# State factors by a product with a 0/1 matrix instead of through DRAM, and a planner that puts wide products between thin ones, in a kernel of linear attention and two dense layers

## The chip, the core and the metric

The kernel runs on one core of a Trainium2 chip. That core has a tensor engine (PE) for matrix products into PSUM, a vector engine (DVE), a scalar engine (ACT), GpSimd (POOL), and a queue on SyncE (SP) from which every transfer of this kernel is issued, in the order of the program. The metric is the time of one launch on the device in microseconds; lower is better.

## What is computed

A linear attention with complex decays feeds a first dense layer, and that a second one. Batch 4, 8 heads, 768 tokens, 48 channels a head; 384 channels in all; hidden widths 2048 and 1536.

```python
mag = np.sqrt(a_re * a_re + a_im * a_im)
scale = np.minimum(mag, 0.999) / (mag + 1e-06)
for t in range(S):
    new_re = ar * S_re - ai * S_im        # ar, ai: the scaled decays of token t
    new_im = ar * S_im + ai * S_re
    S_re, S_im = new_re + einsum('bhd,bhe->bhde', k[t], v[t]), new_im
    y[:, :, t] = einsum('bhd,bhde->bhe', q[t], S_re)
x = y as (tokens, channels)
h = x @ w_in;  x = (h * sigmoid(1.702 * h)) @ w_out              # first layer
g = x @ w_gate;  x = (silu(g) * (x @ w_val)) @ w_out             # second layer
```

## The kernel before, in words

**Tiling.** The attention goes in chunks of 128 tokens. A *unit* is two chunks of one batch, so there are twelve units, u0 to u11, three to a batch; u2, u5, u8 and u11 are the last of theirs. For a unit, DVE and ACT work out running complex products of the decays (`decays`, `products`), then scale queries and keys by them (`queries`: the tile `qh`; `keys`: the line `p<-p,kr`, the last step on DVE). Both go to DRAM (`dq`, `dk`) and come back with the heads' rows in the partitions (`sq`, `sk`; `stack` and `load_heads`). On PE a chunk then takes: transposes of the keys (`kt`), scores (`sc`, 8 heads, in two groups of four, `masked`), the result (`y`, lines 592 and 594, `heads`), its transposes (`xp`, `turn_x`, which make the layer's input `xt`) and what the chunk adds to the state (`ds`). These have 48 or 128 columns and are called *thin* here. At a unit's end the state `M` is multiplied by a real factor for each row of each head, the tile `tots`. The factors `mag` (`passed_on`) lie with channels in the partitions; they go to DRAM as `md` and are read back as `tots`, once for the real and once for the imaginary half.

**The layers.** Weights come as float64 words, which DVE and ACT turn into two float32r parts. For the first 32 blocks of weights the second part is made on PE (lines 773 and 774, an *early pair*). The first layer (`layer_one`) takes 256 tokens, one unit, at a time: 16 blocks `h` of nine products, and 16 blocks `acc` of nine, each `acc` three blocks behind its `h`; between them ACT and DVE make `gs` (`gelu`). The second layer works on 512 tokens at a time (`pg`, `pv`, `o`). The products of both layers have 256 to 512 columns and are called *wide*.

**What sets the order.** `Plan` is a list scheduler that runs while the program is written. Each row of work is a generator that says which engine its next step takes and for how long, and which events or buffer places it waits for. Of the steps that could start first, the one with the smallest urgency number is written next. The numbers come from a table (`URGENCY`, `EXTRA` for each unit, `RUSH`, `W_FIRST`, `SPILL`, `NEAR`). Its times are estimates, and on the chip only the order remains: every engine runs its instructions in that order, and waits where an input is not there. In the program before, a transfer's estimate is 1.3 times its bytes over 360 GB/s plus 3.7 us, a block of nine wide products of 256 columns 1.005 us, and `y` of one chunk is two steps of 1.66 us, between which other work may be put.

```python
for g in range(2):
    yield at[g]
    ...
    yield pe(0.79 if first else 1.66)
    for h in range(4):
        T.matmul(y[:, hs], at[g].x[:, h], u.v[:, c, hs], start=True, stop=first)
        if not first:
            T.matmul(y[:, hs], u.sq[:, 4 * g + h, cols(c)], old[:, hs], start=False, stop=True)
```

Of the kernel before, what the change touches and what calls it, by code (L numbers as in the profile page):

```python
# [30 lines left out]
class Slots:  # L31
    """Places for tiles of one tag, with the times at which they fall free."""
# [5 lines left out]
class Plan:  # L38
    """Puts rows of steps in one order for all engines.

    A row (a generator) asks for what its next step needs: (engine, us), an Event, or Slots; it is
    resumed, and then issues the step. Of the steps that could start first, the one of the most
    urgent row is taken. The times are estimates and only the order rests on them.
    """

    # from the end of a step to the start of one that waits for it
    LAT = {"PP": 0.0, "VP": 0.25, "AP": 0.25, "PV": 0.2, "VV": 0.13, "AV": 0.14, "PA": 0.2, "VA": 0.13, "AA": 0.22}
    # some durations (and those of transfers) are taken long: the order then has slack for them
    SLACK = {"A": 1.05, "V": 1.03}

    def __init__(self):
        self.free = dict(P=0.0, V=0.0, A=0.0, S=0.0, D=0.0)
        self.rows = []
        self.now = 0.0
        self.n = 0
        self.warm = 0.0
        self.table = None
        self.row = [0, 0, None, [], None, "S", NEAR]

    def add(self, urgency, gen, after=False, near=None):  # L60
# [46 lines left out]
    def run(self, until=None):  # L107
        while self.rows and (until is None or until.time is None):
# [4 lines left out]
            for row in self.rows:  # L113
                if isinstance(row[4], tuple):
                    turn = row[4][2:] and row[4][2] != self.table
# [11 lines left out]
            start = self.ready(row, SWITCH if row[4][2:] and row[4][2] != self.table else 0.0)  # L127
            if engine == "P":
                # the tensor engine's clock is at half speed after a pause
                if start - self.free["P"] > (0.5 if start < self.warm else 2.0):  # L130
                    self.warm = start + 3.4
                if start < self.warm:
                    us *= 2
            self.free[engine] = self.now = start + us
# [5 lines left out]
def vec(n):  # L140
    return "V", 0.065 + n / 960
# [6 lines left out]
def act2(n, *table):  # L148
    """Two, the second on what the first gave."""
    return "A", 0.44 + n / 600, *table  # L150

# [4 lines left out]

ISSUE = ("S", 0.48)
NEAR = 0.094
SWITCH = 1.3
TURN = 1018.0  # L160
NEAR0 = [0.129, 0.005]
# [3 lines left out]
class Attention:  # L165
    """Linear attention with complex decays, in chunks of 128 tokens.

    With P[t] the product of a chunk's decays up to t, times the phase of all that came before it
    in the batch, q[t] * P[t] and k[s] / P[s] give the chunk's scores by one product, and the state
    passes from chunk to chunk by real factors (powers of two near the chunk's decay; the phase  # L170
    takes up the rest). A unit is a few chunks of a batch. Channels (h, d) lie in the partitions, in
    NT tiles.
    """

    def __init__(self, nc, plan, const, sb, ps, xs, dram, flag, q, k, v, a_re, a_im, H):
# [10 lines left out]
        make_upper_triangular(nc, self.mask)  # L186
        self.G = None
# [5 lines left out]
    BUFS = dict(p=4, big=2, m2=1, r=1, x=1, d2=1, kr=1, qk=2, v=1, s=1, kn=2, at=2, m=2, sc=2, xt=2, mag=2, tots=1)  # L193
# [4 lines left out]
    def start(self, units):  # L198
        """The rows of work of all units: (batch, first chunk, chunks)."""
        add = self.plan.add  # L200
        for i, (b, c0, n) in enumerate(units):
# [5 lines left out]
                                        "sq", "sk", "tots", "kn", "x", "phase", "md")}  # L207
# [10 lines left out]
    # ---- loads  # L218
# [29 lines left out]
    # ---- decays: a / (|a| + 1e-6) * min(|a|, 0.999)  # L248
    def decays(self, u):
# [11 lines left out]
        # (the logarithm's domain is 2 ** -64 to 2 ** 64)  # L261
# [32 lines left out]
    def root(self, u):  # L294
        """Of the decays' squares."""
# [9 lines left out]
    def inverse(self, u):  # L305
        """Of the products' squares."""
# [9 lines left out]
    # ---- products of the decays over the chunk  # L316
    def cmul(self, out, x, y, shape):
        """out = x * y over complex pairs [128, 2, *shape] (x and y may be broadcast)."""
        V = self.nc.vector
        n = 1  # L320
# [11 lines left out]
        else:  # L332
            full = [128, 2, 2] + list(shape)
            yield vec(4 * n)
# [12 lines left out]
    def products(self, u, last):  # L347
# [8 lines left out]
        # over the blocks of eight: in fours, then over the fours  # L356
# [13 lines left out]
        # G[.., c] is the phase at the start of chunk c of the unit  # L370
# [10 lines left out]
        # the product up to the start of each block of eight  # L381
# [8 lines left out]
        # joined with the products within the blocks  # L390
# [865 lines left out]
```

## Time and profile before

| | |
|---|---|
| median of 3 runs | 1167.28 us (1163.76 to 1175.69) |
| span of the profiled execution | 1167.8 us |
| PE busy | 1096.8 us (94%) |
| PE weight loads | 1015.9 us (87%) |
| DVE busy | 728.8 us (62%) |
| ACT busy | 554.0 us (47%) |
| bytes moved | 103.54 MB, mean 89 GB/s |
| chain that ended last | PE 86%, DMA 7%, DVE 4%, ACT 2% |

Busy is the time in which an engine has an instruction at work. PEclk is the clock that TensorE was granted, as a share of 2.4 GHz; 0.5 is 1.2 GHz. In a list of waits, "PE h L786 <- ACT g" means that PE's instruction of line 786 stood idle until ACT's instruction had written `g`.

### The profile page before, as it was taken

How to read it: one execution, taken by the hardware profiler on the slowest of the kernel's cores; microseconds unless marked ns; L12 is line 12 of the kernel's file. 1: busy time of each engine (PE TensorE's matmuls, PEld its weight loads, DVE VectorE, ACT ScalarE, POOL GpSimd, SP SyncE). 2: the span in 40 equal slices, each digit the busy share in tenths (PEclk: the TensorE clock that was granted, in tenths of full speed). 3: DMA queues.
4: the chain of work that ended last, by engine and by line, in shares of the span. 5: the costliest groups of instructions: out<-in, count | busy, mean ns of one | idle time of the engine just before them, and what ended most of it. 6: DMA issues, size and time to landing. Idle time of an engine off the chain costs nothing.

```text
span 1167.8 us, 18608 instructions
## 1 busy us (share of the span) xinstructions
PE 1096.8 (94%) x7312; PEld 1015.9 (87%) x7312; DVE 728.8 (62%) x1638; ACT 554.0 (47%) x1279; POOL 1.1 (0%) x8
## 2 busy tenths in 40 slices
PE   1549899999999999999999999999999999999996
PEld 0228889999999999999999999888888888888886
DVE  6999988889788998888862599622231231322221
ACT  7987545667447656644442699422121121211211
POOL 0000000000000000000000000000000000000000
PEclk9569999999899999999999999999999999999999
DMA  9770715618257263525813664001010010000000
GB/s 329 251 162 15 164 54 136 159 46 150 82 136 135 70 123 95 122 56 109 163 58 72 211 221 145 27 2 54 1 55 1 1 55 1 28 1 1 28 1 30
DMA packets 101391, 103.54 MB, mean 89 GB/s; under 512 B 14001, under 2 KB 95410, under 8 KB 101298
## 3 DMA queue, kind: packets, MB, share of 16 engines
q1 hardware_dynamic: 101298, 102.29, 34.8%
q8 instruction: 59, 0.97, 0.3%
q14 instruction: 34, 0.28, 0.1%
HBM read 73.95 MB, written 28.32 MB: 88 GB/s over the span
## 4 chain that ended last, share of the span: by engine, by line
PE 86%; DMA 7%; DVE 4%; ACT 2%; issue 1%; SPq 0%; DVEq 0%; ACTq 0%
PE h L786 6%; PE h L788 5%; PE h L787 5%; PE acc L786 5%; PE acc L787 5%; PE acc L788 5%; PE o L1005 4%; PE o L1006 4%; PE o L1007 4%; PE pg L787 4%; PE pv L787 4%; PE pv L786 4%; PE pg L788 4%; PE pg L786 4%; PE pv L788 4%; PE sc L559 4%
## 5 line engine op out<-in xcount | busy, mean ns | idle before, releaser
L975 DVE TENSOR_TENSOR s<-s,pv 128x512 f32<-128x512 f32 x72 | 49.5, 687 | 236.0 <-PE pv L788 234.9
L786 PE MATMUL h<-xt,w 128*128 128x256 f32 x576 | 170.0, 295 | 7.8 <-ACT g L841 6.4
L786 PE MATMUL acc<-gs,w 128*128 128x256 f32 x576 | 169.0, 293 | 0.0
L787 PE MATMUL h<-xt,w 128*128 128x256 f32 x576 | 164.8, 286 | 0.6 <-DVE xt L661 0.6
L787 PE MATMUL acc<-gs,w 128*128 128x256 f32 x576 | 164.5, 286 | 0.4 <-DVE gs L847 0.4
L788 PE MATMUL h<-xt,w 128*128 128x256 f32 x576 | 164.5, 286 | 0.0
L788 PE MATMUL acc<-gs,w 128*128 128x256 f32 x576 | 164.5, 286 | 0.0
L839 ACT ACTIVATE gs<-h 128x256 fp32r<-128x256 f32 x192 | 73.8, 384 | 148.7 <-PE h L788 147.3
L972 ACT ACTIVATE s<-pg 128x512 f32<-128x512 f32 x72 | 43.0, 598 | 174.4 <-PE pg L788 174.4
L786 PEld LDWEIGHTS h<-xt,w 128*128 128x128 f32 x576 | 111.8, 194 | 10.8 <-ACT g L841 8.3
L787 PEld LDWEIGHTS h<-xt,w 128*128 128x128 f32 x576 | 111.9, 194 | 1.0 <-DVE xt L661 1.0
L786 PEld LDWEIGHTS acc<-gs,w 128*128 128x128 f32 x576 | 111.9, 194 | 0.7
L787 PEld LDWEIGHTS acc<-gs,w 128*128 128x128 f32 x576 | 111.8, 194 | 0.7 <-DVE gs L847 0.6
L788 PEld LDWEIGHTS h<-xt,w 128*128 128x128 f32 x576 | 111.8, 194 | 0.0
L847 DVE TENSOR_TENSOR gs<-g,gs 128x256 fp32r<-128x256 f32 x192 | 80.6, 421 | 49.8 <-ACT g L841 48.8
L788 PEld LDWEIGHTS acc<-gs,w 128*128 128x128 f32 x576 | 111.6, 194 | 0.0
L980 ACT CAST p<-s 128x512 fp32r<-128x512 f32 x72 | 44.7, 621 | 130.5 <-DVE s L975 130.5
L1005 PE MATMUL o<-w,p 128*128 128x384 f32 x288 | 97.2, 338 | 0.0
L1006 PE MATMUL o<-w,p 128*128 128x384 f32 x288 | 97.2, 337 | 0.0
L1007 PE MATMUL o<-w,p 128*128 128x384 f32 x288 | 97.1, 337 | 0.0
L787 PE MATMUL pg<-xs,w 128*128 128x512 f32 x216 | 85.1, 394 | 0.0
L787 PE MATMUL pv<-xs,w 128*128 128x512 f32 x216 | 84.7, 392 | 0.0
(128 smaller groups left out, 2448.9 us busy)
## 6 DMA issues: line engine op xcount, KB each, us to landing
words<-in_moe_w_out_dram SPq DMA_DIRECT2D x28, 384.0 KB, 8.4
dq<-qh SPq DMA_DIRECT2D x24, 384.0 KB, 8.9
dk<-p SPq DMA_DIRECT2D x24, 384.0 KB, 6.9
sq<-dq SPq DMA_DIRECT2D x24, 384.0 KB, 7.2
sk<-dk SPq DMA_DIRECT2D x24, 384.0 KB, 8.5
words<-in_moe_w_in_dram SPq DMA_DIRECT2D x16, 384.0 KB, 8.4
p<-in_a_re_dram SPq DMA_DIRECT2D x12, 384.0 KB, 3.8
p<-in_a_im_dram SPq DMA_DIRECT2D x12, 384.0 KB, 4.7
```

What stands on the lines that cost most here:

```text
L559: T.matmul(sc[:, h], u.sk[:, 4 * g + h, cols(c)], u.sq[:, 4 * g + h, cols(c)], start=True, stop=True)
L786: T.matmul(out, w[:, 0, ws], xh, start=start, stop=False)
L787: T.matmul(out, w[:, 0, ws], xl, start=False, stop=False)
L788: T.matmul(out, w[:, 1, ws], xh, start=False, stop=stop)
L839: A.activation(gs[:, 0], h, AF.Gelu_apprx_sigmoid)
L847: V.tensor_tensor(out=gs[:, 1], in0=g, in1=gs[:, 0].bitcast(F32), op=ALU.subtract)
L972: A.activation(s, gv[0], AF.Silu)
L975: V.tensor_tensor(out=s, in0=s, in1=gv[1], op=ALU.mult)
L980: A.copy(p2[:, 0], s)
L1005: T.matmul(os[i], p2[:, 0, cols(i)], w[:, 0], start=f == 0, stop=False)
L1006: T.matmul(os[i], p2[:, 0, cols(i)], w[:, 1], start=False, stop=False)
L1007: T.matmul(os[i], p2[:, 1, cols(i)], w[:, 0], start=False, stop=f == F2 - 1)
```

## The change

It has four parts.

1. **The factors stay on the chip.** Two constants are made on POOL at the start: `rows`, a 0/1 matrix that sends a channel's partition to its row (d, or 48 + d) in the heads' layout, and `mine`, which is 1 where a channel belongs to a head. `passed_on` multiplies `mine` by `mag` on DVE (`own`, bf16, exact since the factors are powers of two), PE multiplies by `rows` (three products of 8 columns into `tp`, each with a weight load of its own), and ACT copies the result to `tots`. The transfers `md<-mag` (one a unit) and `tots<-md` (two a unit) are gone, in the eight units that are not a batch's last.
2. **Wide between thin.** `y` and `ds` are marked as thin steps. The planner adds up the thin time in a row, and where the next thin step would bring it over a limit, it writes another PE step first, if one can start within 0.5 us. Its own estimate of when PE runs at half speed is changed too: from pauses to how much work, thin steps counting for little, it has put there lately.
3. **Other durations.** Transfers are taken at 366 GB/s and 2.5 us, at 1.75 times that for `sq` and `sk`; a block of nine products at 1.08 us; `y` at 1.79, `ds` at 1.36, a group of `sc` at 0.9.
4. **Another table of urgencies**, and the places of weights in SBUF are given out in the order in which they fall free.

```diff
@@ Plan
-    def load(self, event, size):
-        self.free["D"] = max(self.free["D"], self.now + 0.6) + size * 1.3 / 360e3
-        self.set(event, self.free["D"] + 3.1 - self.now)
+    def load(self, event, size, slow=1.0):
+        self.free["D"] = max(self.free["D"], self.now) + size * slow / 366e3
+        self.set(event, self.free["D"] + 2.5 - self.now)
...
+            if row[4][3:] and self.few and self.few + row[4][1] > FEW - 0.6:
+                other = [x for x in ready if x[3][4][0] == "P" and not x[3][4][3:] and x[0] < start + 0.5]
+                if other:
+                    row = min(other, key=lambda x: x[1:3])[3]
...
+                thin = row[4][3:]
+                self.few = (self.few if start - self.free["P"] < 0.3 else 0.0) + us if thin else 0.0
@@ Attention.passed_on
-            yield slots["mag"]
             yield vec(NT)
-            mag = self.tile("mag", [128, NT])
+            mag = sb.tile([128, NT], F32, tag="mag", name="mag", bufs=1)
...
-            yield ISSUE
-            u.md = self.dram.tile([self.HD, 1], F32, tag="md", name="md", bufs=2)
-            self.nc.sync.dma_start(out=u.md.rearrange("(j p) c -> p j c", p=128), in_=mag[:, :, None])
-            plan.set(u.ev["md"], 4.0)
+            if u.c0:
+                yield self.units[u.i - 1].ev["tots"]
+            yield vec(NT * self.H)
+            own = sb.tile([128, NT, self.H], BF16, tag="own", name="own", bufs=1)
+            V.tensor_tensor(out=own, in0=self.mine, in1=mag[:, :, None].to_broadcast([128, NT, self.H]), op=ALU.mult)
+            yield slots["tots"]
+            yield slots["m"]
+            yield pe(0.6)
+            tp = self.tile("m", [128, 512], name="tp", pool=self.ps)[:2 * self.D, :self.H]
+            for j in range(NT):
+                self.nc.tensor.matmul(tp, self.rows[:, j].rearrange("p e d -> p (e d)"), own[:, j],
+                                      start=j == 0, stop=j == NT - 1)
+            yield act(self.H)
+            u.tots = self.tile("tots", [2 * self.D, self.H, 1])
+            A.copy(u.tots[:, :, 0], tp)
@@ Attention.load_heads
-        if not self.last(u, u.n - 1):
-            yield u.ev["md"]
-            yield slots["tots"]
-            yield ISSUE2
-            u.tots = self.tile("tots", [2 * D, H, 1])
-            for e in range(2):
-                self.nc.sync.dma_start(out=u.tots[e * D:(e + 1) * D], in_=u.md.rearrange("(h d) c -> d h c", d=D))
@@ Attention.heads
-                yield pe(0.79 if first else 1.66)
+                yield thin(0.9 if first else 1.79)
...
-                yield pe(1.29)
+                yield thin(1.36)
@@ layer_one, layer_one_out
-                yield pe(9 * N / 2400 + 0.045)
+                yield pe(9 * (N / 2400 + MM))
@@ the table, two of its lines
-W_FIRST, W_STEP = 284.7, 16.205
+W_FIRST, W_STEP = 1731.0, 11.064
```

**Where instructions move.** Lines of the changed kernel have numbers some 50 higher: 592 and 594 (`y`) are 639 and 641, 786 to 788 (the wide products) 835 to 837, 773 and 774 (the early pair) 822 and 823, 742 and 745 (two passes over a weight's words) 790 and 793.

First, PE at the first chunk of u2, where the result of the first four heads ends and that of the other four begins (`at` is the masked scores of one group). Before:

```order
L592 MATMUL y_2054<-v_1629,at_2040 128x48
L594 MATMUL y_2054<-M_1621,sq_1790 128x48
L592 MATMUL y_2054<-v_1629,at_2063 128x48
L594 MATMUL y_2054<-M_1621,sq_1790 128x48
L592 MATMUL y_2054<-v_1629,at_2063 128x48
```

Now, at the same chunk:

```order
L639 MATMUL y_2089<-v_1649,at_2071 128x48
L641 MATMUL y_2089<-M_1636,sq_1758 128x48
L835 MATMUL h_2105<-xt_1494,w_897 128x256
L836 MATMUL h_2105<-xt_1494,w_897 128x256
L837 MATMUL h_2105<-xt_1494,w_897 128x256
...
L639 MATMUL y_2089<-v_1649,at_2085 128x48
L641 MATMUL y_2089<-M_1636,sq_1758 128x48
```

A block of nine wide products has come between the two groups. Before, all 20 chunks that take up a state run their 16 products of `y` without a break; now one of the 20 does, the second chunk of u0.

Second, ACT at the very start, in the decays of u0 (`x` and `r` of 768 columns) and the first weights (`junk`). Before:

```order
L302 ACTIVATE r<-r 128x768
L742 ACTIVATE junk,flags<-words 128x384
L269 ACTIVATE x,flags<-r 128x768
L745 ACTIVATE junk,flags<-junk 128x384
L742 ACTIVATE junk,flags<-words 128x384 x2
L745 ACTIVATE junk,flags<-junk 128x384
L278 ACTIVATE x<-r 128x768
```

Now:

```order
L346 ACTIVATE r<-r 128x768
L313 ACTIVATE x,flags<-r 128x768
L790 ACTIVATE junk,flags<-words 128x384 x2
L793 ACTIVATE junk,flags<-junk 128x384 x2
L322 ACTIVATE x<-r 128x768
L302 ACTIVATE sq,flags<-p 128x1536
L324 ACTIVATE r<-r 128x768
```

The first `x` has moved ahead of the first weight; the second `x` (278, now 322) stands behind two weights' four passes, and the squares of u1 (`sq`) ahead of the last `r`.

Third, PE just before the first wide product, at the end of u0's second chunk. Before:

```order
L773 MATMUL h<-r,ident 128x384
L774 MATMUL h<-w,minus 128x384
L773 MATMUL h<-r,ident 128x384
L774 MATMUL h<-w,minus 128x384
L654 MATMUL xp<-ident,ysb 128x128 x3
L611 MATMUL ds<-v,kn 96x48 x8
L773 MATMUL h<-r,ident 128x384
L774 MATMUL h<-w,minus 128x384
L786 MATMUL h<-xt,w 128x256
```

Now:

```order
L822 MATMUL h<-r,ident 128x384
L823 MATMUL h<-w,minus 128x384
L701 MATMUL xp<-ident,ysb 128x128 x3
L658 MATMUL ds<-v,kn 96x48 x8
L822 MATMUL h<-r,ident 128x384
L823 MATMUL h<-w,minus 128x384
L835 MATMUL h<-xt,w 128x256
```

One early pair has gone from ahead of `xp` to a place further up; there are 32 pairs in both.

## Rows read from the trace of the kernel before

**Rows 1.** Stages: us, busy time of each engine (instructions), PEclk, DMA share, GB/s.
```profile
0.00:84.00 84.00, 33.28 (x63) 15.11 (x63) 70.71 (x173) 71.61 (x200) 1.14 (x8) 0.68 0.83 250
104.50:640.00 535.50, 524.50 (x4370) 518.31 (x4368) 447.46 (x1066) 291.96 (x643) 0.00 (x0) 0.97 0.49 106
640.00:1158.00 518.00, 518.00 (x2741) 464.54 (x2741) 191.44 (x346) 176.00 (x406) 0.00 (x0) 1.00 0.14 47
```
**Rows 2.** The same view, the 10 us in which the granted clock falls.
```profile
140.00:150.00 10.00, 8.09 (x54) 7.47 (x52) 7.31 (x22) 1.55 (x4) 0.00 (x0) 0.83 0.33 86
165.00:175.00 10.00, 7.93 (x51) 7.20 (x49) 9.93 (x18) 6.31 (x12) 0.00 (x0) 0.83 0.46 155
200.00:210.00 10.00, 8.60 (x65) 8.47 (x65) 7.04 (x15) 6.40 (x12) 0.00 (x0) 0.83 0.02 0
250.00:260.00 10.00, 10.00 (x78) 10.00 (x78) 8.07 (x14) 6.38 (x14) 0.00 (x0) 0.83 0.14 41
300.00:310.00 10.00, 10.00 (x65) 10.00 (x65) 5.47 (x13) 3.05 (x8) 0.00 (x0) 0.66 0.01 2
505.00:515.00 10.00, 10.00 (x73) 10.00 (x72) 6.50 (x16) 4.80 (x13) 0.00 (x0) 0.83 0.14 39
630.00:640.00 10.00, 10.00 (x80) 10.00 (x79) 2.83 (x5) 1.72 (x5) 0.00 (x0) 0.83 0.01 2
```
**Rows 3.** The same view, one run of y and the stretch behind it.
```profile
248.90:252.40 3.50, 3.50 (x35) 3.50 (x33) 3.50 (x6) 2.05 (x5) 0.00 (x0) 0.99 0.00 0
252.40:255.80 3.40, 3.40 (x20) 3.40 (x19) 2.05 (x3) 1.68 (x6) 0.00 (x0) 0.51 0.00 0
```
**Rows 4.** PE's waits from 104.5 to 640: us in total, times, longest.
```profile
PE h L786 <- ACT g L841: 6.4, 8, 1.4
PE sc L559 <- DMA sk<-dk: 1.9, 1, 1.9
...
PE h L786 <- ACT xt L659: 0.6, 1, 0.6
```
**Rows 5.** PE products by form: count, busy us, mean ns, idle before.
```profile
L611 PE MATMUL ds<-v,kn 128*96 128x48 f32 x320 | 31.3, 253 | 0.0
```
**Rows 6.** ACT in order of time: start us, us, operation; u0's second x.
```profile
14.72 0.84 ACT L278 ACTIVATE x<-r 128x768 f32<-128x768 f32 x1
```
**Rows 7.** SP's issues of two weights further on, in order of time.
```profile
12.21 0.37 SPq L733 DMA_DIRECT2D words<-in_moe_w_in_dram  x1
...
14.31 0.37 SPq L733 DMA_DIRECT2D words<-in_moe_w_in_dram  x1
```
**Rows 8.** DVE by form, one of a weight's three steps there.
```profile
L753 DVE SCALAR_TENSOR_TENSOR r<-words,r 128x384 int32<-128x384 int32 x68 | 37.3, 552 | 0.4
```
**Rows 9.** PE in order of time: early pairs ahead of xp, and wide products.
```profile
98.57 1.44 PE L773 MATMUL h<-r,ident 128*128 128x384 f32 x2
...
100.12 1.48 PE L773 MATMUL h<-r,ident 128*128 128x384 f32 x2
...
105.07 0.28 PE L788 MATMUL h<-xt,w 128*128 128x256 f32 x1
...
106.15 0.28 PE L788 MATMUL h<-xt,w 128*128 128x256 f32 x1
```
**Rows 10.** SP's issues of keys out and back, u1 and u4.
```profile
123.00 0.89 SPq L447 DMA_DIRECT2D dk<-p  x2
...
132.39 2.91 SPq L503 DMA_DIRECT2D sk<-dk  x2
...
278.72 1.52 SPq L447 DMA_DIRECT2D dk<-p  x2
...
285.82 1.27 SPq L503 DMA_DIRECT2D sk<-dk  x2
```
**Rows 11.** Transfers by line: count, KB each, median us from issue to landing.
```profile
sk<-dk SPq DMA_DIRECT2D x24, 384.0 KB, 8.5
...
tots<-md SPq DMA_DIRECT2D x16, 1.5 KB, 5.2
```

More of the change, by code (lines that the diff above doesn't have):

```diff
@@ L1 @@
 from contextlib import ExitStack
-from itertools import cycle
 import concourse.bass as bass
@@ L55, in __init__, with stretch @@
         self.n = 0
-        self.warm = 0.0
+        self.few = 0.0
+        self.part, self.work, self.cold = 0, 0.0, True
         self.table = None
         self.row = [0, 0, None, [], None, "S", NEAR]
+    def stretch(self, at):
+        while self.part < int(at / STRETCH):
+            self.cold = self.work < 0.35 * STRETCH
+            self.part += 1
+            self.work = 0.0
     def add(self, urgency, gen, after=False, near=None):
@@ L114, in run @@
                 if isinstance(row[4], tuple):
-                    turn = row[4][2:] and row[4][2] != self.table
+                    turn = row[4][0] == "A" and row[4][2:] and row[4][2] != self.table
                     ready.append((self.ready(row), row[0] + (TURN if turn else 0), row[1], row))
@@ L123, in run @@
                 row = min(near, key=lambda x: x[1:3])[3]
+            if row[4][3:] and self.few and self.few + row[4][1] > FEW - 0.6:
+                other = [x for x in ready if x[3][4][0] == "P" and not x[3][4][3:] and x[0] < start + 0.5]
+                if other:
+                    row = min(other, key=lambda x: x[1:3])[3]
             engine, us = row[4][:2]
             us *= self.SLACK.get(engine, 1.0)
-            start = self.ready(row, SWITCH if row[4][2:] and row[4][2] != self.table else 0.0)
+            start = self.ready(row, SWITCH if engine == "A" and row[4][2:] and row[4][2] != self.table else 0.0)
             if engine == "P":
-                if start - self.free["P"] > (0.5 if start < self.warm else 2.0):
-                    self.warm = start + 3.4
-                if start < self.warm:
+                self.stretch(start)
+                if self.cold:
                     us *= 2
+                thin = row[4][3:]
+                self.few = (self.few if start - self.free["P"] < 0.3 else 0.0) + us if thin else 0.0
+                at = start
+                while at < start + us:
+                    self.stretch(at)
+                    end = min(start + us, (self.part + 1) * STRETCH)
+                    self.work += (end - at) * (0.2 if thin else 1.0)
+                    at = end + 1e-9
             self.free[engine] = self.now = start + us
@@ L137, in run, with vec @@
             self.advance(row, next(row[2], None))
[L140 to L141 removed]
+def vec(n, more=0.0):
+    return "V", 0.065 + n / 960 + more
 def act(n, more=0.0, *table):
@@ L150, in act2, with thin @@
     return "A", 0.44 + n / 600, *table
+MM = 0.0135
 def pe(n):
     return "P", n
+def thin(n):
+    return "P", n, None, True
 ISSUE = ("S", 0.48)
-NEAR = 0.094
+NEAR = 0.083
 SWITCH = 1.3
+FEW = 2.9
+STRETCH = 3.413
 TURN = 1018.0
-NEAR0 = [0.129, 0.005]
+NEAR0 = [0.129, 0.072]
 ISSUE2 = ("S", 0.96)
@@ L186, in __init__ @@
         make_upper_triangular(nc, self.mask)
+        self.rows = const.tile([128, self.NT, 2, self.D], BF16, name="rows")
+        nc.gpsimd.memset(self.rows, 0.0)
+        for h in range(H):
+            nc.gpsimd.affine_select(out=self.rows, in_=self.rows, compare_op=ALU.not_equal, fill=1.0, base=-h * self.D,
+                                    pattern=[[128, self.NT], [0, 2], [-1, self.D]], channel_multiplier=1)
+        self.mine = const.tile([128, self.NT, H], F32, name="mine")
+        nc.gpsimd.memset(self.mine, 1.0)
+        nc.gpsimd.affine_select(out=self.mine, in_=self.mine, compare_op=ALU.is_ge, fill=0.0, base=0,
+                                pattern=[[128, self.NT], [-self.D, H]], channel_multiplier=1)
+        nc.gpsimd.affine_select(out=self.mine, in_=self.mine, compare_op=ALU.is_ge, fill=0.0, base=self.D - 1,
+                                pattern=[[-128, self.NT], [self.D, H]], channel_multiplier=-1)
         self.G = None
@@ L504, in load_heads @@
                                        in_=getattr(u, "d" + nm)[e].rearrange("(h d) t -> d h t", d=D))
-            plan.load(u.ev["s" + nm], 1024 * u.F)
-        if not self.last(u, u.n - 1):
-            yield u.ev["md"]
-            yield slots["tots"]
-            yield ISSUE2
-            u.tots = self.tile("tots", [2 * D, H, 1])
-            for e in range(2):
-                self.nc.sync.dma_start(out=u.tots[e * D:(e + 1) * D], in_=u.md.rearrange("(h d) c -> d h c", d=D))
-            plan.load(u.ev["tots"], 0)
-            plan.give(slots["mag"], u.ev["tots"].time - plan.now)
+            plan.load(u.ev["s" + nm], 1024 * u.F, 1.75)
     def last(self, u, c):
@@ L712, in chunked @@
     wp = ctx.enter_context(tc.tile_pool(name="w", bufs=1))
-    wplaces = cycle(range(2 * F1))
+    wplaces = list(range(2 * F1))
     raw = ctx.enter_context(tc.tile_pool(name="raw", bufs=2))
@@ L764, in weight @@
             yield loaded
-            tag = f"w{next(places)}"
+            ev.place = places.pop(0)
+            tag = f"w{ev.place}"
         yield act(DM)
@@ L903, in chunked @@
         w2 = cb.enter_context(tc.tile_pool(name="w2", bufs=1))
-        eplaces = iter(range(extra))
+        eplaces = list(range(extra))
         ps = cb.enter_context(tc.tile_pool(name="ps2", bufs=2, space=PSUM))
```

35 lines of the change are left out of this document (20 added, 15 removed).

## The prediction

> **What bounds the kernel now.** I read first the stages. From 640 us on PE is busy all the time at the full clock, 2.4 GHz [rows 1]: nothing there can be saved, and the change leaves the order of that stretch as it was, but for one block of products. In the first 84 us PE has little to do, while DVE is busy for 70.7 of 84 us [rows 1]: the start is DVE's. Between 104.5 us, the first wide product, and 640, PE is busy for 524.5 of 535.5 us at a mean clock of 0.97 [rows 1]. So what an order can give back there is 11.0 us of idle time and 3% of the clock.
>
> Then I looked at where the clock falls. Seven stretches of 10 us hold all of it [rows 2]: the share missing is 0.17 in six of them and 0.34 in one, so 1.7 us each and 3.4 us for 300 to 310, together 13.6 us. The reader is to see two kinds. From 250 to 260 PE is busy for 10.00 of 10 us and has the clock at 0.83 all the same. The closer look shows a run of `y` from 248.9 to 252.4, PE busy throughout at 0.99, and behind it 3.4 us at 0.51, the lower level, 1.2 GHz [rows 3]. In PE's order of time the spells at 200, 300, 505 and 630 also stand right behind such a run. Those at 140 and 165 don't: ahead of them PE had waited, for `sk` (1.9 us) and for `xt` [rows 4]. The order of the program has 20 such unbroken runs; five were followed by a spell, and no other thin work that PE did without a pause was.
>
> Third, the waits of PE in that stage: 6.4 us for `g` in eight waits, 1.9 for `sk`, 0.6 for ACT's `xt` [rows 4]. No wait for `tots` is among the waits, on PE or DVE.
>
> **The change part by part.** The sum is made against the profiled execution's 1167.8 us, which is 0.5 us above the median of the runs.
>
> *Wide between thin.* In the new order the 16 products of `y` are broken by nine wide products in 19 of the 20 chunks. The longest thin stretch is then one group of four heads, half of a run; `sc` with its eight heads is as long, and no spell stood behind one that PE did without a wait. If the spells come from the unbroken run, those five go: 1.7 + 1.7 + 3.4 + 1.7 + 1.7 = **-10.2 us** [rows 2]. The bounds are 0 and, if the two behind waits go too, -13.6. I take all five, since all five have the same run ahead of them. The one run left is in u0, ahead of the first wide product.
>
> *The spell at 165* came with a wait for `xt` at the start of u1's first layer. Before, `xp` stood right ahead of it; now `ds` and a block of nine wide products, 1.08 us [rows 9], stand between. That covers the wait: **-0.6** for it [rows 4] and **-1.7** for the spell. The spell at 140 I leave, since its wait for `sk` stays.
>
> *The factors' product.* Eight times three products and as many weight loads. The trace has no product of 8 columns. The nearest row is `ds` with 48 columns: 31.3 us for 320 passes, 0.098 each [rows 5]. 21 of the 24 stand on PE's full stretch (the first three fall into the start, where PE is idle anyway): 21 x 0.098 = 2.1. With nothing for them the bound below is 0; with each at its whole 253 ns, not overlapped, it is 5.3. I take 2.1, rounded down to **+1.7** for the fewer columns. The new step on DVE (`own`) is of 24 columns and stands where `mag` was; ACT's copy of 8 columns is hidden, ACT being busy for 292 of 535 us [rows 1]. If they were not hidden, PE would wait at `tp`; but `own` stands 3.3 to 15.7 us of PE's work ahead of it in the orders. POOL's twelve new steps end long before `mine` is used, behind all of u0's decays. The transfers removed are of 1.5 KB, 5.2 us to landing [rows 11], and nothing waited for them: **0**. What they free is the queue between `dk` and the next loads.
>
> *The start.* SP now loads u2's decays ahead of the first weights: two more transfers of 384 KB, at 2.1 us for two [rows 7]. On ACT the first `x` no longer stands behind a weight. But the second `x`, which ran at 14.72 [rows 6], stands behind four passes over two weights that land 2.1 us later, at about 16.1, so the scaled decays of u0 are about 1.5 us late. DVE has one weight more to do ahead of `p<-p,kr`: two steps of 0.55 [rows 8] and a shorter one, with `own` 1.5. Against that, one early pair less stands ahead of the last `xp`, 100.12 - 98.57 = 1.6 us [rows 9], and one load less between `dq` and `dk`, at half of 2.1 some 0.6 if it counted in full for `dk`. Together 1.5 + 1.5 - 1.6 - 0.6 = **+0.8**. The bounds are -2.2 (nothing late) and +3.0 (nothing gained).
>
> *Shorter leads for the keys.* This is the cost that the diff doesn't show. I counted in both orders how much of PE's own work (1.08 us a block [rows 9]) lies between the `h` block whose `gs` DVE does last ahead of a unit's `p<-p,kr` and that unit's first `sc`. Before it was 21.9 to 26.0 us. Now it is 17.6 to 20.1 in u2 to u7 and u9, and 23.6 in u1: 2.2 to 5.0 less in these eight, 29.5 in sum; in u8, u10 and u11 it is 1.5 to 3.2 more. In that time `dk` must land and `sk` must be issued and land. u1 took longest: `dk` issued at 123.00, `sk` at 132.39 and 8.5 to landing [rows 10, 11], over 18 us, and PE waited 1.9. In u4 `dk` to `sk` was 7.1 us [rows 10] instead of 9.4, with `sq` already read; the new order reads `sq` ahead of `dk` in most units. If none had slack, it costs 29.5; if all had 5 us, nothing. Only u1 waited, so the others had some; I take u1's 2.3 and a part of one more unit: **+3.0**.
>
> Sum: 1167.8 - 10.2 - 0.6 - 1.7 + 1.7 + 0.8 + 3.0 = **1160.8**, so 1161.
>
> **The rivals.**
>
> *A. The spells stay.* The new thin stretches still stand close together (`sc`, nine wide, half of `y`, nine wide, half of `y`), and the five spells could come behind these. For it: wide products are a third of PE's time there. Against it: the order before has such neighbourhoods around every `sc` and `ds`, with no spell. The time would be 1161 + 10.2 = 1171. A rule of the Trainium skill points the same way ("TensorE: Matmul & The Clock Gate", HAM oscillation — how this bites in real kernels): what drops the clock is gaps in which PE is idle. By it only the spells behind the two waits are explained, and breaking a run in which PE is busy gives nothing. The trace does not agree, with 10.00 of 10 us busy at 0.83 [rows 2].
>
> *B. Slower: the keys come too late.* In eight units PE would stand at `sc`, since nothing may pass it on PE. It decides where `dk` to the landing of `sk` takes longer than about 15 us in most units, as in u1. Then up to 29.5 instead of 3.0: 1161 + 26.5 = 1187. Against it: the list of waits has one such wait in all.
>
> *C. More than that is saved.* With durations nearer the truth the order could fit everywhere: no new wait for `sk` (-3.0), none of the old one with its spell (-1.9 - 1.7), and half of the waits for `g` gone (-3.2): 1161 - 9.8 = 1151. Against it: the long inserts on ACT between two `g` are about as many in the new order as before, each with two loads of function tables.
>
> *D. It does nothing*: that the factors come by a product instead of a transfer changes no time by itself, as nothing waited for `tots`. That holds in all cases.
>
> **How the numbers follow.** About 1% is what a measurement of this kernel can tell from no change; that is below 1155.6 for faster and above 1179 for slower. My forecast has 0.5, with a range of its own from 1154 to 1167 by the bounds of the start and of the products. A has 0.15, B 0.08, C 0.27. Of the forecast's half, 0.1 lies below 1155.6; C lies there with all its 0.27; so 0.37 faster. B is slower, 0.08. The rest is 0.55. The range goes from 1148, C with its start at the lower bound, to 1173, A with 2 us more of waits; B and a little of C are left out.
>
> **What would show it.** In the changed kernel the stretches of 10 us between 200 and 640 should have the clock at 1.00, but behind a wait; `sc <- DMA sk` among PE's waits should be some 5 us and not 20; the first wide product should start within 104 to 108 us; from the end of the heads on nothing should differ. The forecast is wrong if spells come behind halves of `y`, if `sk` is waited for in more than two or three units, or if DVE's start slips by more than 3 us.

## The result, and the profile after

| | before | changed |
|---|---|---|
| median of the runs, us | 1168.64 (1163.76 to 1175.69, 4 runs) | 1151.81 (1151.36 to 1152.83, 4 runs) |
| profiled execution's span, us | 1167.8 | 1150.1 |
| first wide product starts, us | 104.5 | 102.5 |
| DMA packets | 101391 | 91792 |

The ratio is 0.985, with a 95% interval from 0.982 to 0.989; beside three other kernels it was 0.987 (0.982 to 0.991). Ratios, here and below, leave out executions over 1.5% above the fastest of their kernel, while medians take all in. So the change is faster by 1.5%, some 17 us, or 14.5 beside those three. That is 9 us below the forecast of 1161 and just the number of rival C, 1151. The times of the changed kernel also lie closer together, within 1.5 us instead of 12.

The stages of the changed kernel (us, busy time and instructions of PE, PEld, DVE, ACT, POOL, granted clock, DMA share, GB/s), to set against [rows 1]:

```profile
0.00:84.00 84.00, 34.83 (x76) 16.24 (x77) 70.57 (x175) 72.18 (x204) 5.62 (x20) 0.84 0.79 249
104.50:640.00 535.50, 528.07 (x4527) 522.70 (x4526) 455.71 (x1085) 303.44 (x681) 0.00 (x0) 1.00 0.44 113
640.00:1141.00 501.00, 501.00 (x2594) 447.14 (x2593) 183.59 (x332) 165.89 (x376) 0.00 (x0) 1.00 0.12 40
```

The reader is to see the clock of the middle stage, 1.00 for 0.97, and the idle time there: 535.5 - 528.1 = 7.4 us instead of 11.0. Four of the seven stretches of [rows 2] in the same view:

```profile
140.00:150.00 10.00, 10.00 (x86) 9.47 (x85) 8.65 (x33) 2.60 (x8) 0.00 (x0) 1.00 0.00 0
165.00:175.00 10.00, 9.06 (x75) 9.04 (x76) 9.55 (x19) 4.87 (x15) 0.00 (x0) 1.00 1.08 267
250.00:260.00 10.00, 10.00 (x89) 9.90 (x89) 9.96 (x19) 9.85 (x18) 0.00 (x0) 1.00 0.95 233
300.00:310.00 10.00, 10.00 (x85) 9.90 (x84) 9.75 (x18) 4.23 (x12) 0.00 (x0) 1.00 1.07 264
```

All seven are at the full clock, those behind waits too. PE's waits from 104.5 to 640 (us in total, times, longest), to set against [rows 4]:

```profile
PE h L835 <- ACT g L891: 4.1, 5, 1.7
PE h L835 <- ACT tots L494: 2.3, 2, 1.6
PE acc L836 <- DVE gs L897: 0.6, 1, 0.6
PE h L836 <- DVE xt L708: 0.2, 1, 0.2
```

From 104.5 on there is no wait for `sk` any more, though the way from the keys to the scores got shorter. The two waits put down to `tots` are waits for `g`: ACT's own copy of 8 columns takes 0.16 us and stands behind two loads of function tables of 1.28 us each. So 6.4 us of waits for `g` are what they were. What had changed in the transfers I had not looked for (line, count, KB, median us from issue to landing); of before:

```profile
dq<-qh SPq DMA_DIRECT2D x24, 384.0 KB, 8.9
dk<-p SPq DMA_DIRECT2D x24, 384.0 KB, 6.9
...
md<-mag SPq DMA_DIRECT2D x8, 1.5 KB, 10.5
```

and of the changed kernel, where `sk` is to be set against [rows 11]:

```profile
dq<-qh SPq DMA_DIRECT2D x24, 384.0 KB, 3.7
dk<-p SPq DMA_DIRECT2D x24, 384.0 KB, 4.9
...
sk<-dk SPq DMA_DIRECT2D x24, 384.0 KB, 5.5
```

The transfers of queries and keys land 2 to 5 us sooner. From the issue of `dk` to that of `sk` it was 7.2 us on the mean of the twelve units before (6.9 in u0, 8.3 in u11) and is 4.9 (2.9 and 3.4); with the landing of `sk` that makes 15.7 us before and 10.4 now.

Of the 17.7 us between the two profiled executions, rows account for 17.4: 13.6 of clock, 3.6 of idle time, 2.0 of the start, less 1.8 for the products. The experiments ask what brought each.

### The profile page after: what moved, and what is told of

It reads as the page before. It is cut to its first block, busy times and chain, and to the rows that moved or that the text cites. A ratio compares the mean times of both kernels' runs of the same rounds, so it can differ in the third digit from the quotient of the medians.

```text
span 1150.1 us, 18650 instructions
## 1 busy us (share of the span) xinstructions
PE 1083.8 (94%) x7336; PEld 1002.6 (87%) x7336; DVE 730.8 (64%) x1646; ACT 555.4 (48%) x1289; POOL 5.6 (0%) x20
## 2 busy tenths in 40 slices
DMA packets 91792, 103.51 MB, mean 90 GB/s; under 512 B 4401, under 2 KB 85810, under 8 KB 91698
## 3 DMA queue, kind: packets, MB, share of 16 engines
q1 hardware_dynamic: 91698, 102.26, 31.5%
## 4 chain that ended last, share of the span: by engine, by line
PE 83%; ACT 6%; DVE 5%; DMA 4%; issue 1%; SPq 1%; DVEq 0%; ACTq 0%
PE h L835 6%; PE acc L835 5%; PE h L836 5%; PE h L837 5%; PE acc L836 5%; PE acc L837 5%; PE o L1058 4%; PE o L1056 4%; PE o L1057 4%; PE pg L836 4%; PE pv L836 4%; PE pv L835 4%; PE pg L837 4%; PE pg L835 4%; PE pv L837 4%; PE sc L606 3%
## 5 line engine op out<-in xcount | busy, mean ns | idle before, releaser
L835 PEld LDWEIGHTS h<-xt,w 128*128 128x128 f32 x576 | 110.0, 191 | 11.0 <-ACT g L891 6.5
L836 PEld LDWEIGHTS acc<-gs,w 128*128 128x128 f32 x576 | 110.3, 191 | 0.8 <-DVE gs L897 0.8
L836 PEld LDWEIGHTS h<-xt,w 128*128 128x128 f32 x576 | 110.1, 191 | 0.6 <-DVE xt L708 0.6
L835 PEld LDWEIGHTS acc<-gs,w 128*128 128x128 f32 x576 | 110.1, 191 | 0.1
L837 PEld LDWEIGHTS acc<-gs,w 128*128 128x128 f32 x576 | 110.1, 191 | 0.0
L837 PEld LDWEIGHTS h<-xt,w 128*128 128x128 f32 x576 | 109.9, 191 | 0.0
```

The costliest lines, as they stand in the source:

```text
L835: T.matmul(out, w[:, 0, ws], xh, start=start, stop=False)
L836: T.matmul(out, w[:, 0, ws], xl, start=False, stop=False)
L837: T.matmul(out, w[:, 1, ws], xh, start=False, stop=stop)
```

## The experiments

Every kernel below moves or adds only what its diff says; the order of all other instructions on each engine is kept word for word. (The planner still reckons as it did; only what it issues at a step is exchanged.) That is what makes them comparable, since a new plan would change the whole order. The kernel before, beside them, had medians of 1169.4, 1166.8 and 1166.9 us in the three groups; the changed kernel, run again in the last, 1152.4. Differences to the changed kernel are mostly between groups, and the medians of the kernel before differ by up to 2.5 us between groups, so these differences are known to some 3 us.

### Wide between thin

**y's run made whole again.**

```diff
-                for h in range(4):
-                    hs = cols(4 * g + h, D)
-                    T.matmul(y[:, hs], at[g].x[:, h], u.v[:, c, hs], start=True, stop=first)
+                for h in range(8 if g else 0):
+                    hs = cols(h, D)
+                    T.matmul(y[:, hs], at[h // 4].x[:, h % 4], u.v[:, c, hs], start=True, stop=first)
```

> The changed kernel with one thing moved: the first half of y's products is issued at the place of the second half, so that a chunk's 16 products stand in one run again (20 runs, as before the change) and the nine wide products that broke them stand ahead. Nothing else moves on any engine. Theory 1 (the low clock comes behind unbroken thin runs): spells of low clock return in some of the runs, 3 to 8 of them at 1.7 us, so 5 to 13 us more than the changed kernel's 1151.8: 1157 to 1165, and a wider scatter of the times. Theory 2 (the spells came behind waits, and the new order has fewer of them): no spell more, 1151 to 1154.

Measured: 1161.0 us (1157.2 to 1168.1), 9.2 more than the changed kernel; ratio to before 0.993 (0.989 to 0.996). The view of stretches, a run of `y` and what is behind it:

```profile
391.60:395.30 3.70, 3.70 (x35) 3.70 (x34) 3.70 (x8) 3.63 (x5) 0.00 (x0) 1.00 0.00 0
395.30:398.70 3.40, 3.40 (x18) 3.40 (x18) 3.13 (x6) 1.04 (x4) 0.00 (x0) 0.51 0.86 278
```

It is [rows 3] again: PE busy throughout, 1.00 in the run and 0.51, the lower level, right behind it. From 104.5 on such spells stood behind 4 of 19 runs, one of them double, 8.5 us together, and one stood ahead of the first wide product. PE's waits from 104.5 to 640 came to 7.3 us, where the changed kernel has 7.2. So theory 1 holds. The rule that I had set against it (the Trainium skill, "TensorE: Matmul & The Clock Gate", HAM oscillation — how this bites in real kernels), by which the clock falls after gaps in which PE is idle, does not cover these spells: in the run ahead of this one PE was busy for 3.70 of 3.70 us.

**y's run split in the kernel before.** Three of the nine wide products ahead of the run are issued at once, the other six held back and issued behind `y`'s first half; any other work on PE ahead of it releases them. So it comes about in 16 of 20 chunks:

```diff
+                wide(range(1))
+                plan.held = wide
...
                         T.matmul(y[:, hs], u.sq[:, 4 * g + h, cols(c)], old[:, hs], start=False, stop=True)
+                plan.flush()
```

> The kernel before with one thing moved: in 16 of the 20 chunks the last six of the nine wide products that stood ahead of y's run are issued between its halves (the first three stay between sc and y). Nothing else moves on any engine. Theory 1: the spells behind y go where it is split: 1168.6 less 8 to 10, so 1158 to 1161. Theory 2: they stay, 1167 to 1170, or some 2 more where y's first half waits for its masked scores.

Measured: 1164.4 us (1162.9 to 1173.3), ratio 0.996 (0.993 to 0.998): 5 us less, not 8 to 10. The stretches show where the rest stayed:

```profile
200.00:210.00 10.00, 8.60 (x69) 8.47 (x69) 7.03 (x15) 7.66 (x16) 0.00 (x0) 0.89 0.08 9
250.00:260.00 10.00, 10.00 (x79) 10.00 (x79) 8.07 (x15) 6.31 (x14) 0.00 (x0) 0.83 0.14 41
300.00:310.00 10.00, 10.00 (x94) 10.00 (x93) 8.50 (x19) 5.55 (x12) 0.00 (x0) 1.00 0.01 2
...
630.00:640.00 10.00, 10.00 (x91) 10.00 (x90) 2.69 (x6) 2.83 (x8) 0.00 (x0) 1.00 0.12 41
```

300, 505 and 630 are clean. At 250 stands one of the four runs that stayed whole, and its spell stayed. At 200 the run is split and a spell is there all the same, with a wait for `g` of 1.4 us; from 160 to 180, behind waits for `xt` and `g` of 2.9 us, the clock is at 0.67 and 0.82. So there are two kinds, as I had read, but the one at 200 I had put down to the wrong kind. Why a wait of 1.4 us is followed by a spell here, and one of 1.7 us (for `g` at 166) by none in the changed kernel, the runs don't show.

### The factors' transfers

**Through DRAM again, in the new order.** The store stands where `own` stood, the loads behind those of `sk`:

```diff
-            V.tensor_tensor(out=own, in0=self.mine, in1=mag[:, :, None].to_broadcast([128, NT, self.H]), op=ALU.mult)
+            self.nc.sync.dma_start(out=u.md.rearrange("(j p) c -> p j c", p=128), in_=mag[:, :, None])
...
-                self.nc.tensor.matmul(tp, self.rows[:, j].rearrange("p e d -> p (e d)"), own[:, j],
-                                      start=j == 0, stop=j == NT - 1)
...
-            A.copy(u.tots[:, :, 0], tp)
...
+                self.nc.sync.dma_start(out=u.tots[e * D:(e + 1) * D], in_=u.md.rearrange("(h d) c -> d h c", d=D))
```

> The changed kernel with the factors through DRAM again: one store of 128 x 3 where the step own stood, two loads behind sk's; the 24 products, own and the copy of tots are gone, all else keeps its place on each engine. Theory 3 (the factors' transfers, of four bytes a piece, slow those that stand near them): dk and sk take as long as before, some 15.7 us from dk's issue to sk's landing on the mean instead of 10.3, while the new order leaves 13.7 to 16.6 us between dk's issue and the first sc in most units: waits for sk of 1 to 2 us in four to six units, 5 to 10 us in all, less 2.1 for the products: 1155 to 1160. Theory 4 (the transfers got shorter because the order of the loads around them changed): no waits for sk, and the products' 2 us are saved: 1149 to 1151.

Measured: 1177.2 us (1174.2 to 1181.5), ratio 1.009 (1.006 to 1.012). That is 25 us more than the changed kernel and slower than before, far beyond what theory 3 expected. SP's issues of u1 in this kernel, in order of time (start us, us):

```profile
117.40 0.37 SPq L484 DMA_DIRECT2D md<-mag  x1
119.06 0.90 SPq L497 DMA_DIRECT2D dq<-qh  x2
...
130.08 0.84 SPq L553 DMA_DIRECT2D sq<-dq  x2
131.01 1.57 SPq L497 DMA_DIRECT2D dk<-p  x2
137.69 1.52 SPq L553 DMA_DIRECT2D sk<-dk  x2
```

and in the changed kernel:

```profile
113.31 0.90 SPq L503 DMA_DIRECT2D dq<-qh  x2
...
119.24 0.94 SPq L559 DMA_DIRECT2D sq<-dq  x2
120.61 1.18 SPq L503 DMA_DIRECT2D dk<-p  x2
127.55 2.06 SPq L559 DMA_DIRECT2D sk<-dk  x2
```

Behind the store of `md`, `dq` takes 11.0 us to where `sq` can be issued, instead of 5.9. DVE has the keys ready at the same distance as ever, but `dk` stands behind `sq` in SP's order and goes out 6.5 us after DVE began on it instead of 1.8. What the engines moved meanwhile (columns as in [rows 1]): in this kernel with the store alone under way, and then with `dq`, `q` and `k` behind it,

```profile
118.00:119.00 1.00, 1.00 (x11) 1.00 (x10) 1.00 (x2) 0.99 (x2) 0.00 (x0) 1.00 0.20 2
122.00:127.00 5.00, 4.61 (x38) 4.61 (x39) 5.00 (x8) 1.75 (x6) 0.00 (x0) 1.00 0.77 14
```

and in the changed kernel with `dq` and `q`:

```profile
114.00:118.00 4.00, 2.43 (x18) 1.83 (x17) 4.00 (x10) 2.98 (x6) 0.00 (x0) 1.00 0.93 290
```

The store's own packets show as 0.20 us of all 16 engines; behind it the transfers moved at 14 GB/s instead of 290, until about the time at which it landed (10.1 us from its issue, on the median).

PE then stood at `sc` for 11.9 us in five places between 100 and 640, with spells of low clock behind three of them; the first `sc` came at 87.7 instead of 83.2 and the first wide product at 108.2 instead of 102.5.

**The product in the old order.** `own` stands behind `mag`, the products behind a unit's last `ds`, in spare columns of its PSUM tile:

```diff
+                    for j in range(NT):
+                        T.matmul(tp, self.rows[:, j].rearrange("p e d -> p (e d)"), u.own[:, j],
+                                 start=j == 0, stop=j == NT - 1)
...
+                        V.tensor_copy(u.tots[:, :, 0], tp)
```

> The kernel before with the factors by a product: own stands behind mag on DVE, the three products stand behind the unit's last ds and write spare columns of its bank, DVE copies them ahead of M's sum; the store and the loads are gone, all else keeps its place. Theory 3: sk lands in some 5.5 us instead of 8.5, the one wait for sk in u1 (1.9 us) goes with the spell behind it (1.7), the products cost 2.1: 1166 to 1168. Theory 4: landing times as before, 2 us more: 1170 to 1171.

Measured: 1163.1 us (1161.7 to 1171.6), ratio 0.995 (0.992 to 0.998), 6 us less: more than theory 3 expected, though the products were paid for. The wait for `sk` is gone; `dk` lands in 5.0 us for 6.9. But `sk` itself lands in 7.9 us for 8.5, not in the 5.5 that I expected, and with the transfers back in the new order it took 5.3: the 3 us by which `sk` lands sooner in the changed kernel are the new order's, not the store's. The same removal is worth 6 us in an order where the scores come 15.2 to 21.9 us after `dk`, and 25 in one where they come 12.8 to 16.6 us after it in ten of the twelve units.

**The store alone, and the loads alone**, added to the changed kernel beside its product, the store behind `own`, the loads (of a tile `md` stored once) behind those of `sk`:

```diff
+            self.nc.sync.dma_start(out=u.md.rearrange("(j p) c -> p j c", p=128), in_=mag[:, :, None])
```

> The changed kernel, product and all, with the old store of mag to DRAM added where own stands, 128 x 3 values of four bytes, eight times; nothing reads it. Theory 5 (the store takes over 10 us to land and holds dq, dk and sq, which stand behind it in the queue, by 5 to 6 us): most of the 25 us that the transfers of the factors cost in this order come back, 1168 to 1177, with waits for sk in the units in which the store stands ahead of dq or dk. Theory 6 (the loads of the factors cost it, or both together): 1152 to 1158.

> The changed kernel with the two old loads of the factors (48 x 8 values of four bytes each) added behind sk's, into a tile that nothing uses, from a DRAM tile that is stored once in the first unit. Theory 5: the loads stand behind all that is urgent; beside the one store in the first unit, which can cost the start some 4 us, nothing: 1152 to 1157. Theory 6: 1160 or more.

Measured: 1182.7 us with the store (1179.6 to 1190.0), 1159.2 with the loads (1157.5 to 1164.6). Both lie above theory 5's ranges, the loads just below theory 6's 1160. Of the 6.4 us by which the profiled execution with the loads is longer than the changed kernel's, 6.1 are there at the first wide product (108.6 for 102.5), behind the one store in u0: the first `sc` comes at 87.6, and the clock is at 0.65 and 0.84 from 80 to 100. Behind the first wide product the waits are the changed kernel's to 0.2 us. So it is the store, as theory 5 said. q1's packets took 33.8% of the 16 engines' 1182.3 us with the store and 31.5% of 1150.1 without it, 37 us more for eight stores. Nearly all of that must be packets of transfers beside the store, held up, since its own took some 0.2 us above. The queue's line, with the store and without it:

```profile
q1 hardware_dynamic: 94898, 102.27, 33.8%
```

```profile
q1 hardware_dynamic: 91698, 102.26, 31.5%
```

**The store behind sk.** The kernel with the factors through DRAM, its store moved from where `own` stood to between the loads of `sk` and of `tots`:

```diff
-            self.nc.sync.dma_start(out=u.md.rearrange("(j p) c -> p j c", p=128), in_=mag[:, :, None])
...
+            self.nc.sync.dma_start(out=u.md.rearrange("(j p) c -> p j c", p=128), in_=u.mag[:, :, None])
```

> The changed kernel with the factors through DRAM (no product), as in the experiment that put them back, but with the store issued behind sk's loads instead of ahead of dq and dk; the loads of the factors stand right behind it and wait for it. Theory 5: the time is that of the changed kernel or the products' 2 us less, 1149 to 1154, with no wait for sk; the product is then one way among others of taking the store out of the keys' way. If small transfers slow their neighbours wherever they stand, 1158 or more.

Measured: 1165.5 us (1161.1 to 1169.8), ratio 0.999 (0.995 to 1.002): no gain over the kernel before, and outside the range of theory 5. The keys' transfers are as short as with the product (`dk` 4.7 us, `sk` 5.7), but PE waits 6.3 us for `ysb` in two places. In this kernel SP issues the store at 223.44 and the loads of `tots` only at 231.57, when it has landed; behind them stand the next unit's decays, for which ACT then waits, with `ysb` queued behind:

```profile
238.42 1.48 ACT L302 ACTIVATE sq<-p 128x1536 f32<-128x1536 f32 x1 [7.56 <-DMA p<-in_a_im_dram]
239.81 0.19 ACT L302 ACTIVATION_READ_ACCUMULATOR sq<-p 128x1 f32 x1
239.90 0.47 ACT L645 ACTIVATE ysb<-y 128x384 f32<-128x384 f32 x1
```

While SP waits there for the store, the DMA engines show no packet at all (columns as in [rows 1]):

```profile
228.00:231.50 3.50, 2.09 (x19) 1.92 (x17) 1.96 (x11) 1.36 (x5) 0.00 (x0) 1.00 0.00 0
```

And q1's packets, the same eight stores among them, took 31.2% of 1163.3 us, 363 us for the changed kernel's 362. So a store that is not yet landed does not keep the engines busy. It holds up what is issued behind it; by what means, the trace does not show. My expectation named the keys and forgot what else stands in that queue. Half of theory 5 held.

**The same store in other pieces, and from another engine.** First 128 pieces of 12 bytes for 384 of 4:

```diff
-            self.nc.sync.dma_start(out=u.md.rearrange("(j p) c -> p j c", p=128), in_=mag[:, :, None])
+            self.nc.sync.dma_start(out=u.md.rearrange("(p j) c -> p (j c)", p=128), in_=mag)
```

> As the changed kernel with the added store (1182.7 us), at the same place of the queue and with the same wait for mag, but laid out so that each partition's three values go to DRAM as one piece: 128 pieces of 12 bytes instead of 384 of 4. Theory 7 (the cost goes by the number of small pieces): the store lands in 4 to 6 us instead of 10.6, and a third of the 30 us stays, 1158 to 1165. Theory 8 (the queue stands still for the wait on mag, whatever is stored): 1178 to 1184.

Then 128 pieces of 512 bytes:

```diff
+            V.tensor_tensor(out=row, in0=self.mask, in1=mag[:, :1].to_broadcast([128, 128]), op=ALU.mult)
+            self.nc.sync.dma_start(out=u.md, in_=row)
```

> As before at the same place of the queue, but 64 KB in 128 pieces of 512 bytes (a 128 x 128 tile that DVE makes from mag, 0.2 us eight times on DVE). Theory 7: it lands in some 3 us and costs next to nothing, 1152 to 1157, though it is over 40 times the bytes. Theory 8: 1178 to 1184. If any store ahead of the keys costs its own landing: in between, about 1160.

Then the factors through DRAM again, without the product, the old store and the old loads issued by GpSimd, the loads now right behind the store instead of behind `sk`:

```diff
+            self.nc.gpsimd.dma_start(out=u.md.rearrange("(j p) c -> p j c", p=128), in_=mag[:, :, None])
...
+                self.nc.gpsimd.dma_start(out=u.tots[e * self.D:(e + 1) * self.D], in_=u.md.rearrange("(h d) c -> d h c", d=self.D))
```

> The changed kernel without the product: the old store and the old loads of four-byte pieces, but issued by GpSimd, which has nothing else to do by then, so that no transfer of SP's queue stands behind them and nothing on SP waits for the store to land. If it is the place in SP's queue that costs: no wait for sk and none for the factors, and the products' 2 us are saved: 1149 to 1152. If the small pieces hold the DMA engines themselves, whichever queue they come from: 1165 to 1180.

Measured: 1156.2 us (1153.1 to 1161.1 in eight executions, a ninth took 2759.9), 1154.5 (1151.0 to 1159.8) and 1193.5 (1190.6 to 1195.9), with ratios of 0.991, 0.990 and 1.022. The stores' landing in the three, in that order:

```profile
md<-mag SPq DMA_DIRECT2D x8, 1.5 KB, 2.2
```

```profile
md<-row SPq DMA_DIRECT2D x8, 64.0 KB, 2.3
```

```profile
md<-mag POOLq DMA_DIRECT2D x8, 1.5 KB, 10.4
```

The first has the same bytes, the same place and the same wait for `mag`, and costs 4 us instead of 31, less than theory 7 expected: it is not the place in SP's order, and theory 8 falls. It is how the 1.5 KB are cut, 384 pieces of four bytes. From GpSimd these do the same harm to SP's transfers: `sq` of u1 is issued 11.9 us after `dq`, and PE waits 20.4 us for `sc`. The queues of that run, SP's and GpSimd's:

```profile
q1 hardware_dynamic: 91698, 102.26, 33.5%
q0 software_dynamic: 768, 0.04, 0.2%
```

SP's queue has the changed kernel's 91698 packets and none of the factors' pieces, and they took 33.5% of 1188.8 us, 36 us more than there. So the store holds up transfers of another queue too, whoever issues it. That agrees with a sentence of the Trainium skill ("DMA: Bandwidth & Descriptors", Issuing engines are not separate DMA queues): all issuers' transfers end on the same 16 engines. How much of the 1193.5 us is the store's and how much that of the moved loads isn't told apart; in u1 the loads go out only at 131.33, when `dq`, issued at 121.62, had been held already. My expectation that GpSimd's queue could beat the product was wrong.

**Both parts by hand in the old order.** The two diffs above on the kernel before:

> The kernel before with both parts done by hand and its own order otherwise kept: the factors by a product, and y's run split in 16 of 20 chunks. If the two parts add up: 6.2 and 5.0 less than before, so 1157 to 1159, and what is left to the changed kernel's 1151.8 is the new order's (its shorter way from the keys to the scores). If the spells that waits brought go as well once sk comes in time: 1152 to 1155.

Measured: 1162.0 us (1159.6 to 1163.8), ratio 0.994 (0.992 to 0.997), hardly less than the product alone and above both of my ranges. The stretches at 300, 390, 500, 590, 600 and 630 are at 1.00. What is left are the spells at the start (0.83, 0.87 and 0.96 from 80 to 110), behind waits (160 to 180 and 200) and at 250, behind the run that stayed whole. The changed kernel has none of these: its order starts the wide products 1.3 us sooner (102.5 for 103.7), has 2.9 us less of idle time, and covers the waits for `xt`. So about 10 us come only with the new order, and it has them only because the store is gone: with it, 1177. Which of the order's two sources brings them, the other durations or the other table, no run separates.

> The changed kernel itself, beside the three above: 1151 to 1153.

Measured: 1152.4 us (1152.3 to 1153.1).

## Why the prediction was right or wrong

The range held the time; the likeliest number was 9 us too high, and the outcome is "faster by over 1%", which had 0.37. Step by step:

**Wide between thin, -10.2: right.** Undone in the changed kernel it costs 9.2. The reading that the run does it, against the rule on idle gaps, stood the test in both directions, with 5 us for 8 to 10 in the old order. Only the spell at 200 was of the other kind. That five runs were struck in the execution I read is in part luck: with the product in the old order, stretches of unbroken work at 0.83 stood at 390, 500, 590, 600 and 640, and none at 250, 300 and 630.

**The spell at 165, -0.6 and -1.7: right in the sum.** The wait for `xt` is gone and the clock is at 1.00. But a wait for `g` of 1.7 us stands there now, which brought no spell.

**The factors' product, +1.7: right.** Of the products of 8 columns:

```profile
L490 PE MATMUL tp<-own,rows x24: 166/186/223, 62.4 to 543.7; 128*96 128x8 bf16 x24
```

Three of them take 0.26 us in a row, 0.087 each where I had 0.098 for 48 columns. Seven groups on the full stretch make 1.8.

**The transfers removed, 0: this is the step that failed.** I priced them by who waits for them, and by the loads' 5.2 us. The store's 10.5 us stood in the same view of before, and I passed it over, because nothing waited for it. It held up what stands behind it: `dq`, `dk`, `q` and `k` (8.9, 6.9, 8.6 and 7.2 us to landing before, 3.7, 4.9, 4.2 and 3.5 in the changed kernel, on the median). It was worth 6 us in the old order and 25 in the new one. Rival D, of which I wrote that it holds in all cases, is refuted.

**Shorter leads for the keys, +3.0: wrong by its sign, in good part from the same cause.** I had counted the leads rightly (`dk` to the first `sc` is 12.8 to 16.6 us in ten of the twelve units), but set against them the pace of u1 of before, which had the store in it ("over 18 us"; the rows named make 9.4 + 8.5 = 17.9). With 10.4 us for the way, every unit has slack. Of the 5.3 us between that and the 15.7 of before, some 3 are `sk`'s landing, which the new order brought; that too I had not counted. So the wait for `sk` (1.9) and the spell behind it (1.7), which I had left in place, went too. With the store in place the time comes near my rival B's, 1177 to 1183 where I had 1187, but not by B's way: PE stood at `sc` for 11.9 us in five places (15.2 with the product beside the store), not in eight units, because `dk` went out late, behind `sq`. The start and the spells made up the rest.

**The start, +0.8: it was -2.0.** The late `x` and the added weight are there: `p <- p, kr` of u0 stands at 68.7 instead of 66.7 (the row is of DVE in order of time). But from `dk` to the first `sc` it takes 12.8 us instead of 15.7, and the early pairs between that and the first wide product are fewer. The first is the store only together with the order: put back in the new order it makes 18.0, taken out of the old one it leaves 15.2. What I had not counted at all is the clock: from 84 to 104.5 it was 0.89 and is 1.00, which is 2.3 us. Why, no run shows. With the transfers in place the start slipped by 3.7 us (108.2 for 104.5), just beyond my upper bound of 3.0.

**The rivals.** C gave the number, 1151, in part by luck, since it named the durations as the cause and not the store. Two of its three terms came: no wait for `sk`, no spell with it. Its third, half of the waits for `g`, didn't come (6.4 us as before). The rest was the start. A is refuted by the clock of 1.00. So the forecast missed not a rival but a cause: the part of the change that its own words put first, and that I had set at nothing.

## What to carry to other kernels

A transfer that nobody waits for is not free: read its time to landing and how fast the transfers behind it move until then, and list these before removing it is priced at nothing. A price counted from leads holds only for the pace of the transfers after the change; if an edit takes something out of their way, count that first. Where a clock falls while the engine is busy, look at what kind of work ran just before, not only at waits.

## What the runs showed of the hardware

**Pieces of four bytes.** A store to DRAM of 1.5 KB in 384 pieces of 4 bytes took 10.5 us to land, and the transfers issued behind it moved at 14 GB/s instead of 290 meanwhile; the store's own packets were some 0.2 us of all 16 DMA engines. The same bytes in 128 pieces of 12 took 2.2 us, and 64 KB in 128 pieces of 512 took 2.3. Loads of four-byte pieces, 768 in two transfers, landed in 3.8 to 6.0 us and, behind `sk`, cost the kernel little. The Trainium skill ("DMA: Bandwidth & Descriptors", Specifications) gives 512 bytes as the least size for full rate, with a read, a change and a write below it. In the time to landing of 128 pieces these runs show no step between 12 and 512 bytes, with over 40 times the bytes; what step there is lies between 4 and 12, or between 384 and 128 pieces, or in their order in DRAM (the four-byte pieces of neighbouring partitions are neighbours there, those of one partition 512 bytes apart). Which of these it is wasn't told apart.

**The clock behind busy work.** PE fell from 2.4 to 1.2 GHz for 3.4 us, once for about twice as long, right behind runs of products of 48 columns in which it never paused, in some of them only (4 of 19 in one execution). Half a run between wide products brought none in the changed kernel. What decides which of the whole runs it strikes stays open.
